# Two last units turned on TensorE, one product group in another PSUM ring, and a new order table, in an mLSTM and SoLU kernel

## The chip, the cores and the metric

The kernel runs on one core of one Trainium2 chip. The metric is the time of one execution in device microseconds (us), taken as the median of several runs; smaller is better.

## The reference

Two layers follow each other. The first is an mLSTM cell over 4 batches, 8 heads, 768 time steps and a head width of 40; the second is a feed-forward layer on the 3072 resulting rows of 320 numbers.

```python
for t in range(S):                                    # per batch and head
    m_new = np.maximum(f_gate[:, :, t] + m, i_gate[:, :, t])
    f_stab, i_stab = np.exp(f_gate[:, :, t] + m - m_new), np.exp(i_gate[:, :, t] - m_new)
    C = f_stab * C + i_stab * outer(vt, kt)
    n = f_stab * n + i_stab * kt
    y[:, :, t] = sigmoid(o_gate[:, :, t]) * (C @ qt) / np.maximum(np.abs(n @ qt), 1.0)
x = y.transpose(0, 2, 1, 3).reshape(B * S, H * D)     # 3072 x 320
h = x @ w_in                                          # 320 -> 1024
solu = h * softmax(h)
ln = (solu - mean(solu)) / np.sqrt(var(solu) + 1e-6) * g_ln
out = ln @ w_out                                      # 1024 -> 320
```

## The kernel before

**Units.** The 768 steps are cut into 6 chunks of 128. A unit is one chunk of one batch, with all 8 heads: 24 units, ordered by chunk and inside a chunk by batch. So unit u needs the state that unit u - 4 left. Inside a chunk the recurrence is written as attention: scores of the chunk's own keys, a decay matrix, and a term from the state.

**One unit, step by step, with the names used below.** TensorE multiplies keys and queries (line 1280, tile `sy`, called e). VectorE multiplies the scores by the decay matrix `d` (line 1293, `p`). TensorE adds the term from the state (line 1320, y.0; VectorE scales it in line 1333) and the products of `p` with the values (line 1347, y.1 and y.2) in one bank. VectorE divides (lines 1363 to 1371, `x`), GpSimd multiplies by the output gate (line 1383), ScalarE takes a row sum of magnitudes (1392), VectorE a scale (1398, 1399), and ScalarE and GpSimd split the row into two fp16 halves `xq` (1453 to 1467). A DMA transpose turns `xq` to `xT` (line 1481). TensorE forms h in `ph` (lines 1497 and 1511, called ph.0 to ph.3). VectorE takes the maximum (1527, `nm`; 1534, `nh`), ScalarE the exponentials (1541), VectorE the product (1559), and ScalarE and VectorE write the centred result as a high and a low fp16 half, `us` (1595 and 1602). `us` is turned into `big`: in units 0 to 22 by one DMA transpose (line 1611), in unit 23 alone by TensorE, 8 transposes for each half (line 1476) into a bank of the ring `sy`, which VectorE (high half, 1626) and ScalarE (low half, 1624) copy to `big`. TensorE multiplies by the output weights: 24 matmuls of 320 columns (line 1664, so.0 to so.3, six each) into the bank `so_`. ScalarE scales the result (line 1680, `ot`) and a DMA stores it (1685).

**PSUM.** The ring `sy` has three banks, in which e, y and the turned halves take turns by a place number; `ph` has two buffers of two banks; `so_` has one bank, which the state updates (line 1416) and the output products share. A group of output products can start only when ScalarE has taken the one before out of that bank.

**The weights.** In the first 75 us the float64 words of both weight matrices are decoded on ScalarE and VectorE (lines 792 to 827), scaled by a bound found through a TensorE transpose (lines 893 and 1031; VectorE's part of the second begins in line 1026, `wmx`), and split into a high and a low fp16 part (lines 935 to 945, 1060 and 1070, `wol`).

**The order.** Every step is a numbered operation of a `Plan`. The table `ORDER` gives the sequence in which all operations are issued, so it fixes the order on each engine and on SP, which issues all DMAs. A pair `(a, b)` interleaves the matmuls of two TensorE operations, and a triple `(a, -1, n)` puts n idle matmuls ahead of a. An engine runs its own operations strictly in that sequence and waits, with all that stands behind, until the inputs of the next one are there. State and value products of the first 6 units that are not in a pair also get an idle matmul beside each step (line 1705).

Of the kernel before, what the change touches and what calls it, by code (L numbers as in the profile page):

```python
# [39 lines left out]
def gdv(P):  # L40
# [433 lines left out]
def mlstm_moe_kernel(ctx: ExitStack, tc: tile.TileContext, tok, qkT, og, fi0, fg, ig, w_in, w_out, gln, out):  # L474
    nc = tc.nc
    units = unit_order()
    NU = len(units)
# [8 lines left out]
    P = Plan()  # L486
# [630 lines left out]
    def unit(u):  # L1117
# [17 lines left out]
        def bank(name, at, ring="sy"):  # L1135
            k = (ring, (name, u))
            P.place[k] = u + at
            return k
# [439 lines left out]
        def uTv(P, a):  # L1578
            return P[uT].bitcast(F16)[:, 0 : 2 * DFF].rearrange("p (a k l) -> p a k l", a=2, l=L)[:, a]


        last = u == NU - 1
        mu = ("mu", u)
        op(
            DVE,
# [173 lines left out]
```

## Time and profile before

| what | us |
|---|---|
| median of 3 runs | 292.49 |
| the three runs | 290.56, 292.49, 297.13 |
| the profiled execution | 291.3 |
| its span | 289.6 |
| TensorE (PE) busy | 275.9 (95%) |
| VectorE (DVE) busy | 231.4 (80%) |
| ScalarE (ACT) busy | 218.3 (75%) |
| GpSimd (POOL) busy | 165.4 (57%) |

The span runs from the first to the last instruction of the profiled execution; its time is 1.7 us longer. PE is TensorE's matmuls, PEld its weight loads, SP the engine that issues the DMAs. A matmul's end is modelled, so TensorE counts as busy through gaps shorter than its pipeline. A time that names a moment is counted from the start of the span.

### The profile page before, as it was taken

Reading aid. Unit: us, or ns where it says so; the run is one execution under the profiler, and the core shown is the slowest. Engines: PE = TensorE matmul, PEld = TensorE weight load, DVE = VectorE, ACT = ScalarE, POOL = GpSimd, SP = SyncE. Lnnn points to the kernel's source line nnn. Section 1 sums busy time; section 2 is a strip of 40 time slices with the busy share of each in tenths; the row PEclk is TensorE's granted clock in tenths of the full one; section 3 lists DMA queues with packets and bytes.
Section 4 is the critical chain, followed back from the end, with each engine's and each line's share of the span. In section 5 each row is a group of like instructions: output and inputs, shape, how many; then the busy total and the mean of one; then the engine's idle time right before and its main releaser. Section 6 shows DMA issues by size and latency. Waiting matters only on the chain.

```text
span 289.6 us, 6648 instructions
## 1 busy us (share of the span) xinstructions
PE 275.9 (95%) x2299; PEld 214.1 (74%) x2299; DVE 231.4 (80%) x611; ACT 218.3 (75%) x472; POOL 165.4 (57%) x275
## 2 busy tenths in 40 slices
PE   6999798998999999999999999999999999989884
PEld 6977787776868878767778777887887767755563
DVE  1999997999988799968789769988897996749720
ACT  2489968989399987799576749997988559466632
POOL 5005879856377388876754476489277326643050
PEclk9999999999999999999999999999999999999999
DMA  7999968587999999699999999969958996496531
GB/s 192 326 336 370 273 169 235 192 244 167 265 221 198 278 261 263 143 239 182 279 252 240 200 288 206 208 161 240 262 177 189 194 231 123 100 155 131 118 79 45
DMA packets 87521, 61.02 MB, mean 211 GB/s; under 512 B 70096, under 2 KB 77392, under 8 KB 87488
## 3 DMA queue, kind: packets, MB, share of 16 engines
q1 hardware_dynamic: 87488, 60.61, 86.3%
q8 instruction: 18, 0.29, 0.4%
q14 instruction: 15, 0.12, 0.1%
HBM read 39.16 MB, written 4.26 MB: 150 GB/s over the span
## 4 chain that ended last, share of the span: by engine, by line
PE 65%; DVE 15%; issue 8%; POOL 4%; ACT 4%; DMA 4%; ACTq 0%; POOLq 0%; DVEq 0%
PE ph L1511 20%; PE sy L1347 6%; PE sy L1280 6%; PE sy L1320 4%; DVE p L1293 3%; DMA big<-us 2%; PE ph L1497 2%; ACT d L1211 2%; DMA xT<-xq 1%; DVE wol L1070 1%; DVE wg L816 1%; DVE wg L827 1%; PE so__4047 L1664 1%; PE so__4086 L1664 1%; PE so__3556 L1664 1%
## 5 line engine op out<-in xcount | busy, mean ns | idle before, releaser
L1664 PEld LDWEIGHTS <-big 128*128 128x128 f16 x576 | 63.2, 116 | 20.5 <-issue 2.4
L1347 PEld LDWEIGHTS sy<-tk,p 128*128 128x128 f32 x384 | 58.0, 193 | 8.9 <-DVE p L1293 2.1
L1511 PE MATMUL ph<-wih,xT 128*128 128x512 f16 x192 | 60.3, 380 | 0.0
L1347 PE MATMUL sy<-tk,p 128*128 128x41 f32 x384 | 57.2, 242 | 2.7 <-DVE p L1293 1.7
L1211 ACT ACTIVATE d<-gb,bG 128x128 f32<-128x128 f32 x160 | 50.0, 391 | 2.4 <-POOL kt L1262 2.4
L1511 PEld LDWEIGHTS <-xT 128*128 128x128 f16 x336 | 36.9, 114 | 18.8 <-issue 2.8
L1511 PE MATMUL ph<-wil,xT 128*128 128x512 f16 x144 | 48.5, 380 | 0.0
L1460 POOL TENSOR_TENSOR xs<-x,xr 128x320 f32<-128x320 f32 x24 | 18.4, 768 | 32.0 <-DVE xr L1399 22.0
L1383 POOL TENSOR_TENSOR x<-x,sg 128x320 f32<-128x320 f32 x24 | 21.7, 905 | 25.8 <-DVE x L1371 15.4
L1541 ACT ACTIVATE e<-ph,nh,hs 128x1024 f32<-128x1024 f32 x24 | 28.7, 1198 | 8.4 <-DVE nh L1534 8.3
L1559 DVE SCALAR_TENSOR_TENSOR e<-ph,s,e 128x1024 f32<-128x1024 f32 x24 | 30.7, 1281 | 4.8 <-ACT e L1541 4.3
L1527 DVE TENSOR_REDUCE nm<-ph 128x1 f32<-128x1024 f32 x24 | 29.2, 1216 | 4.6 <-PE ph L1511 4.6
L1293 DVE TENSOR_TENSOR p<-sy,d 128x512 f32<-128x512 f32 x48 | 32.1, 683 | 0.8 <-POOL d L1233 0.3
L1602 DVE SCALAR_TENSOR_TENSOR us<-e,mu,us 128x1024 f16<-128x1024 f32 x24 | 31.7, 1320 | 0.3 <-ACT us L1595 0.3
L1320 PEld LDWEIGHTS sy<-C,qk 128*128 128x128 f32 x160 | 28.0, 190 | 4.8 <-issue 1.3
L1595 ACT ACTIVATE us<-e,mu 128x1024 f16<-128x1024 f32 x24 | 27.4, 1142 | 2.8 <-DVE mu L1587 2.8
L1320 PE MATMUL sy<-C,qk 128*128 128x82 f32 x160 | 27.6, 260 | 0.7 <-DVE x L1371 0.7
L1569 ACT ACTIVATE sq<-e,a 128x1024 bf16<-128x1024 f32 x24 | 27.4, 1141 | 0.0
L1280 PE MATMUL sy<-qk 64*128 64x128 f32 x384 | 27.3, 281 | 0.0
L1467 POOL TENSOR_TENSOR xq<-xs,xq 128x256 f16<-128x256 f32 (+1 forms) x48 | 25.6, 554 | 2.3 <-ACT xq L1453 1.6
L1280 PEld LDWEIGHTS sy<-qk 64*128 64x128 f32 x384 | 23.8, 187 | 3.3 <-issue 1.7
L1196 POOL TENSOR_SCALAR_AFFINE_SELECT gb<-gb 128x1024 f32<-128x1024 f32 x20 | 22.7, 1133 | 3.3 <-DMA gb<-gd 3.2
(268 smaller groups left out, 614.5 us busy)
## 6 DMA issues: line engine op xcount, KB each, us to landing
gb<-gd SPq DMA_DIRECT2D x20, 512.0 KB, 4.7
qk<-in_qkT_dram SPq DMA_DIRECT2D x21, 448.0 KB, 5.4
tk<-in_tok_dram SPq DMA_DIRECT2D x24, 324.0 KB, 3.8
sg<-in_og_dram SPq DMA_DIRECT2D x12, 320.0 KB, 7.2
out_dram<-ot SPq DMA_DIRECT2D x24, 160.0 KB, 3.6
big<-in_w_in_dram SPq DMA_DIRECT2D x5, 512.0 KB, 7.1
big<-in_w_out_dram SPq DMA_DIRECT2D x4, 640.0 KB, 4.8
qk<-in_qkT_dram SPq DMA_DIRECT2D x3, 512.0 KB, 6.8
```

Of the source, the lines that this page charges most:

```text
L1211: nc.scalar.activation(out=P[d_t][:, j, n, :], in_=P[gb][:, h, :], func=AF.Exp, bias=P[BG][:, 0, c - 1, b * H + h : b * H + h + 1],)
L1280: nc.tensor.matmul(P[ps[j]][:, n * L : (n + 1) * L], lhsT=P[qk][r, 1, n, :], rhs=P[qk][r, 0, n, :], start=True, stop=True,)
L1293: lambda P, j=j: V.tensor_tensor(out=P[p_t][:, j], in0=P[ps[j]].rearrange("p (n l) -> p n l", l=L), in1=P[d_t][:, j], op=ALU.mult,),
L1320: nc.tensor.matmul(P[yk][:, n * 2 * E1 : (n + 1) * 2 * E1], lhsT=P[qk][:, 0, n, :], rhs=P[old][:, n, :], start=first_of_bank(), stop=False ...
L1347: nc.tensor.matmul(yv(P)[:, h, :], lhsT=P[p_t][:, j, n, :], rhs=v1(P)[:, h, :], start=first_of_bank(), stop=True, skip_group_check=True,)
L1511: nc.tensor.matmul(P[ph][:, j * 512 : (j + 1) * 512], lhsT=P[xT][:, a, :], rhs=P[w][:, k, j * 512 : (j + 1) * 512], start=False, stop=n == 6,)
L1527: lambda P: V.tensor_reduce(out=P[nm], in_=P[ph], axis=AX.X, op=ALU.max, negate=True),
L1541: lambda P: nc.scalar.activation(out=P[e], in_=P[ph], func=AF.Exp, bias=P[nh], scale=P[hs], accum_out=P[z]),
L1559: lambda P: V.scalar_tensor_tensor(out=P[e], in0=P[ph], scalar=P[s2], in1=P[e], op0=ALU.mult, op1=ALU.mult, accum_out=P[a]),
L1569: lambda P: nc.scalar.activation(out=P[sq], in_=P[e], func=AF.Square, bias=P[a], scale=-float(DFF), accum_out=P[su]),
L1602: lambda P: V.scalar_tensor_tensor(out=P[us][:, 1], in0=P[e], scalar=P[mu], in1=P[us][:, 0], op0=ALU.add, op1=ALU.subtract),
L1664: nc.tensor.matmul(P[po][:, 0:DM], lhsT=uTv(P, a)[:, k, :], rhs=P[w][:, k, :], start=n == 0, stop=n == 23)
```

## The change

Units 22 and 23 are both turned by TensorE; before, unit 22 was turned by a DMA. Unit 23's output products go to a bank of the ring `sy`, so they no longer wait for unit 22's to leave the bank `so_`. The place numbers of the turned halves are moved so that they fall in sequence. `ORDER` is another list throughout; its first rows stand here for the whole.

```diff
 ORDER = [
-    202, 34, 250, 5, 3, 0, 18, 297, 17, 19, 40, 46, 2, 31, 132, 155, 52, 1, 4, 136, 35, 7, 58, 8, 6, 11, 20, 41, 9,
+    3, 34, 297, 155, 5, 32, 17, 250, 18, 0, 40, 6, 1, 46, 31, 132, 19, 52, 4, 58, 35, 7, 8, 36, 20, 41, 37, 11, 9, 21,
...
-        last = u == NU - 1
+        last = u >= NU - 2
...
-                up = bank(f"t{a_}", 0.4 + 0.1 * a_)
+                up = bank(f"t{a_}", NU - 1 - u + 0.4 + 0.1 * a_ + (0.2 if u == NU - 1 else 0.0))
...
-        po, ot = (("so_", u), ("ot", u))
-        P.place[po] = u + 4.5
+        ot = ("ot", u)
+        po = bank("po", 0.9) if u == NU - 1 else ("so_", u)
+        if u < NU - 1:
+            P.place[po] = u + 4.5
...
+                name="so_",
```

On TensorE the sequence from unit 7 to unit 21 stays nearly the same. At the end it was: products of unit 20, of unit 21, high half of unit 23 turned, products of unit 22, low half of unit 23 turned, products of unit 23. Now it is: products of unit 20, both halves of unit 22 turned, products of unit 21, both halves of unit 23 turned, and then the products of units 22 and 23 six by six among each other (22, 23, 22, 23, 23, 22, 22, 23). The four quarters of unit 19's products, which stood between the four parts of unit 23's h, now stand ahead of them.

VectorE at the very start of the program, where `gb` holds the gates of the first chunk (loaded by a DMA) and `ident` is made by GpSimd. Before:

```order
L563 SCALAR_TENSOR_TENSOR gb<-gb 128x128
L577 TENSOR_TENSOR gb<-gb 128x127
L548 TENSOR_REDUCE dl<-ident 128x8
L555 TENSOR_REDUCE ra<-ident 128x1
L555 TENSOR_REDUCE rb<-ident 128x1
L601 TENSOR_TENSOR gb<-gb 128x128
```

VectorE at the same place now:

```order
L548 TENSOR_REDUCE dl<-ident 128x8
L555 TENSOR_REDUCE ra<-ident 128x1
L555 TENSOR_REDUCE rb<-ident 128x1
L563 SCALAR_TENSOR_TENSOR gb<-gb 128x128
L577 TENSOR_TENSOR gb<-gb 128x127
L800 TENSOR_SCALAR e<-wt 128x512
```

The three sums over `ident` moved ahead of the scan of the gates.

VectorE around the bound of the output weights (`wmx`), where `wg` is the last part of those weights to be decoded and `C` the state. Before:

```order
L827 SCALAR_TENSOR_TENSOR wg<-big,wg 128x640
L1398 TENSOR_SCALAR xm<-xm 128x1
L1399 RECIPROCAL xr<-xm 128x1
L1405 TENSOR_SCALAR hs<-xm,iwi 128x1
L1445 COPY C_72<-so__549 40x4x41
L1026 TENSOR_REDUCE wmx<-wm 128x1
```

VectorE at the same place now:

```order
L827 SCALAR_TENSOR_TENSOR wg<-big,wg 128x640
L1445 COPY C_483<-so__474 40x4x41 x2
L1363 TENSOR_SCALAR rd<-sy 128x8
L1364 TENSOR_TENSOR rd<-sy,rd 128x8
L1365 RECIPROCAL rd<-rd 128x8
L1398 TENSOR_SCALAR xm<-xm 128x1
L1399 RECIPROCAL xr<-xm 128x1
L1371 TENSOR_TENSOR x<-sy,rd 128x320
L1293 TENSOR_TENSOR p<-sy,d 128x512 x2
L1445 COPY C_82<-so__547 40x4x41
L1026 TENSOR_REDUCE wmx<-wm 128x1
```

The decoding of the last part moved ahead of unit 2's division, of unit 3's two score products and of the states of units 1 and 2.

ScalarE at the end of the program, where `ot` with a number is the scaled output of units 20 to 23 in turn. Before:

```order
L1680 ACTIVATE ot<-so__3934,so 128x320
L1569 ACTIVATE sq,su<-e,a 128x1024
L1595 ACTIVATE us<-e,mu 128x1024
L1569 ACTIVATE sq,su<-e,a 128x1024
L1680 ACTIVATE ot<-so__3983,so 128x320
L1680 ACTIVATE ot<-so__4047,so 128x320
L1624 COPY big<-sy 128x1024
L1680 ACTIVATE ot<-so__4086,so 128x320
```

ScalarE at the same place now:

```order
L1569 ACTIVATE sq,su<-e,a 128x1024 x2
L1541 ACTIVATE e,z<-ph,nh,hs 128x1024
L1683 ACTIVATE ot<-so__3930,so 128x320
L1595 ACTIVATE us<-e,mu 128x1024
L1683 ACTIVATE ot<-so__3995,so 128x320
L1624 COPY big<-sy 128x1024
L1569 ACTIVATE sq,su<-e,a 128x1024
L1624 COPY big<-sy 128x1024
L1683 ACTIVATE ot<-so__4064,so 128x320
L1683 ACTIVATE ot<-sy,so 128x320
```

A second copy of a turned half stands behind unit 21's output, and the squares of units 21 and 22 moved ahead of unit 23's exponentials.

## Rows read from the trace of the kernel before

**Rows 1.** Busy time by stretch: us, PE, PEld, DVE, ACT, POOL, granted clock, DMA, GB/s.

```profile
30.00:73.00 43.00, 38.39 (x364) 31.55 (x363) 39.75 (x106) 37.09 (x88) 32.86 (x42) 1.00 0.78 210
73.00:254.00 181.00, 180.52 (x1504) 139.76 (x1503) 151.37 (x414) 142.70 (x314) 113.67 (x191) 1.00 0.96 216
254.00:273.00 19.00, 18.19 (x115) 10.72 (x114) 13.12 (x36) 12.06 (x20) 6.19 (x12) 1.00 0.62 131
273.00:286.50 13.50, 11.17 (x88) 7.87 (x87) 4.03 (x9) 6.14 (x10) 4.14 (x8) 1.00 0.32 77
```

**Rows 2.** Waits of PE from 24 to 73: who waited for whom, total, times, longest.

```profile
PE sy L1347 <- DVE p L1293: 1.7, 2, 1.3
PE ph L1031 <- DVE wmx L1028: 1.1, 1, 1.1
PE sy L1320 <- DVE x L1371: 0.7, 1, 0.7
PE sy L1347 <- DVE sy L1333: 0.7, 2, 0.4
```

**Rows 3.** Waits of PE from 254 to the end.

```profile
PE so__4047 L1664 <- DMA big<-us: 1.0, 1, 1.0
PE so__3983 L1664 <- ACT ot L1680: 0.8, 1, 0.8
PE ph L1497 <- DMA xT<-xq: 0.8, 1, 0.8
PE so__4086 L1664 <- ACT ot L1680: 0.2, 1, 0.2
```

**Rows 4.** Timeline, DVE at the start: start, us, engine, line, operation, [idle before <- releaser].

```profile
6.03 0.42 DVE L563 TENSOR_TENSOR_SCAN gb<-gb 128x128 f32<-128x128 f32 x1 [6.03 <-DMA gb<-in_fi_dram]
...
6.70 0.26 DVE L548 TENSOR_REDUCE dl<-ident 128x8 f32<-128x64 f32 x1
...
7.06 0.28 DVE L601 TENSOR_TENSOR gb<-gb 128x128 f32<-128x128 f32 x1
...
24.15 0.69 DVE L1293 TENSOR_TENSOR p<-sy,d 128x512 f32<-128x512 f32 x1 [0.33 <-POOL d L1233]
```

**Rows 5.** Timeline, DVE from 42 to 68.

```profile
42.16 1.47 DVE L827 SCALAR_TENSOR_TENSOR wg<-big,wg 128x640 int32<-128x640 int32 x1
...
44.58 0.16 DVE L1026 TENSOR_REDUCE wmx<-wm 128x1 f32<-128x4 f32 x1 [0.36 <-ACT wj L1008]
...
47.85 0.51 DVE L1333 TENSOR_TENSOR sy<-sy,bG 128x328 f32<-128x328 f32 x1 [1.20 <-PE sy L1705]
...
67.34 1.38 DVE L1070 SCALAR_TENSOR_TENSOR wol<-wg,gs,woh 128x320 f16<-128x320 f32 x1
```

**Rows 6.** The chain that ended last, its end: start, us, what.

```profile
272.45 6.06 DMA big<-us
278.56 3.45 PE so__4047 L1664 x24
282.08 0.54 ACT ot L1680
282.66 3.43 PE so__4086 L1664 x24
286.25 0.53 ACT ot L1680
```

**Rows 7.** Timeline, all engines, from 269 to 283.

```profile
269.52 0.30 PE L1664 MATMUL so__3934<-woh,big 128*128 128x320 f16 x1
...
271.11 1.28 DVE L1602 SCALAR_TENSOR_TENSOR us<-e,mu,us 128x1024 f16<-128x1024 f32 x1
...
276.95 0.61 PE L1476 MATMUL sy<-ident,us 128*128 128x128 f16 x8
...
277.60 0.69 DVE L1626 COPY big<-sy 128x1024 f16<-128x1024 f16 x1 [0.23 <-PE sy L1476]
...
282.50 1.00 ACT L1624 COPY big<-sy 128x1024 f16<-128x1024 f16 x1
```

126 rows, old and new, of the table ORDER are left out of this document.

## The prediction

> **What bounds the kernel now.** I read the busy time by stretch first [rows 1]. From 73 to 254 TensorE is busy for 180.52 of 181.0 us: there is nothing to take in this stretch but TensorE's own work, and the change leaves that work alone. Only three stretches have room. From 30 to 73 TensorE is idle for 43.00 - 38.39 = 4.6 us while VectorE is busy for 39.75, so VectorE limits the start. From 254 to 273 TensorE is idle for 0.8 us, and from 273 to 286.5 for 13.50 - 11.17 = 2.3 us, of which some 0.3 lie behind its last matmul. The views of waits name the causes. At the start TensorE waits for VectorE's score products (1.7 us in two waits, one of 1.3), for the bound of the output weights (1.1), for unit 6's division (0.7, `x`) and for the scaling of the state term (0.7) [rows 2]. At the end it waits for the DMA that turns unit 22 (1.0), for ScalarE to empty the one bank of output products (0.8 and 0.2) and for one `xT` (0.8) [rows 3]. So if every wait after 30 us went, and 1.2 us of new work (below) came in, the gain would be 4.6 + 0.5 + 0.8 + 2.0 - 1.2 = 6.7 us. With 0.5 us by which the first score product can start earlier, that is the floor: 291.3 - 7.2 = 284.1 us. The reader should keep this small number in mind: a new order for 1340 operations cannot give more than this.
>
> The sums are made against the profiled execution's 291.3 us. It lies 1.2 us below the median of the three runs, 292.49, and 0.7 above the lowest.
>
> **The start of the program.** VectorE waited 6.03 us for the gates' DMA, and then did three sums over `ident` between the scan of the gates and its next step: they begin at 6.70 and the next step begins at 7.06 [rows 4]. Now they stand ahead of the scan and fall into the wait, since `ident` is long made. That takes 7.06 - 6.70 = 0.36 us out of the path to the first score product, which at 24.15 also waited 0.33 us for GpSimd [rows 4]. The set of VectorE operations ahead of that product is the same in both orders, and the last decoding step that ScalarE must see before it makes the first decay matrix stands earlier in VectorE's row. I take 0.5 us; the bounds are 0 (ScalarE or the loads are late instead) and 0.36 + 0.33 = 0.7.
>
> **The bound of the output weights.** Before, the last decoding step ran from 42.16 for 1.47 us, ScalarE had to sum its result, and VectorE waited 0.36 us for that sum at 44.58 [rows 5]. TensorE stood still for 1.1 us because its next operation needs this bound [rows 2], and as its row is strict, unit 4's state term came late and VectorE then waited 1.20 us for it at 47.85 [rows 5]. Now two score products (0.69 us each [rows 4]), a division and copies of two states stand between the decoding step and the bound, where four short steps stood, so VectorE comes to the bound at least 1.4 us later after the decoding and ScalarE's sum is ready. The bound itself has four steps fewer ahead of it and one more. What hides ScalarE's sum is this VectorE work; if ScalarE slipped by over 1 us, the 0.36 us would come back. I take the whole 1.1 us of TensorE's wait, bounds 0 and 1.1 + 0.4.
>
> **From 45 to 73.** VectorE has one `wol` step fewer ahead of unit 6's division, a step that took 1.38 us at that place [rows 5], and one row scale fewer; so the wait of 0.7 us for that division [rows 2] should go. The step comes back right behind, ahead of unit 7's products, but there TensorE has output products to do. The two waits of 0.7 us for the scaling, and what is left of the 1.7 us for score products, I leave standing: VectorE is still the limit there. Unit 4's state update is now interleaved with a part of h, which saves four idle matmuls; TensorE waits in this stretch anyway, so I count nothing. Sum of the start: 0.5 + 1.1 + 0.7 = 2.3 us, bounds 0 and 4.6 + 0.7 = 5.3.
>
> **The stretch from 73 to 254.** TensorE's row is nearly the same, and so are the distances in it between a unit's last value product, its h and its output products. VectorE, ScalarE, GpSimd and SP are reordered throughout. Here I count 0, with bounds of -0.5 (both of its small waits go) and +4 (the rival below). At 256 TensorE waited 0.8 us for unit 22's `xT` [rows 3]. Two quarters of unit 17's output products (12 matmuls, 1.6 us) moved behind the first part of that h, so TensorE asks for this `xT` 1.6 us sooner; against that the output of unit 16, which ScalarE must finish ahead of unit 22's `xq`, can start sooner too, since its last products moved ahead of two parts of unit 21's h. I take no change, with 0.8 us either way.
>
> **The end.** The work that TensorE does ahead of unit 20's output products is the same set in both orders, so I start at 269.52 [rows 7]. One matmul of the products comes every (3.45 - 0.30) / 23 = 0.137 us [rows 6, 7]. Before: 96 of them are 13.15 us, two turned halves of 0.61 each [rows 7] are 1.2; 269.52 + 14.4 = 283.9, but the last group ended at 282.66 + 3.43 = 286.1 [rows 6]: 2.2 us of waits, of which rows 3 name 1.0 + 0.8 + 0.2. Now: 13.15 plus four halves, 2.4, give 285.1, if nothing waits. Each group after unit 20's has 1.2 us of transposes ahead of it, which cover ScalarE's 0.54 us for emptying the bank [rows 6]; the DMA of 6.06 us [rows 6] is gone from this path, and with it one transpose from SP's row, in which four stores stood behind it. Unit 23's products have a bank of their own.
>
> What may be late instead: unit 22's low half, which VectorE began at 271.11 and finished 1.28 us later [rows 7], is asked for at about 269.5 + 3.3 + 0.6 = 273.4; in the new row the short steps for unit 23 come first, and about 0.5 us of margin is left. Unit 23's group waits for a bank of the ring that ScalarE frees with its 1.00 us copy [rows 7], behind unit 21's output; that copy ends within some 0.2 us of the time at which the bank is asked for, and behind the waiting matmuls stands all the rest of unit 22. I allow 0.1 us for both: a gain of 286.1 - 285.1 - 0.1 = 0.9 us, bounds -1.0 (a slip of one ScalarE operation on each group) and 1.0. The last output (0.53 us) and its store follow as before.
>
> **Sum.** 291.3 - 2.3 - 0.9 = 288.1 us for an execution like the profiled one, 289.3 on the scale of the median. I forecast 288.6, between the two.
>
> **A rule that speaks against the turn on TensorE.** The rows show that 8 transposes took 0.61 us and that TensorE's granted clock was 1.00, the upper level of 2.4 GHz, through the whole stretch from 273 to 286.5, although TensorE both waited and turned two halves there [rows 1, 7]. The Trainium skill ("TensorE: Matmul & The Clock Gate", Part 4: PE-mode transpose) says that transposes do not count as activity for the clock in the same way as matmuls, and that one of 128x128 took 275 to 390 ns where it was measured. By its 275 ns the four halves would cost an estimated 8.8 us; by the row they cost 2.4, and this trace does not agree with the page's duration. What it says of the clock is a rival below, since the change doubles the transposes.
>
> **Rivals.**
> - *The start does not move (0.20).* VectorE is 92% busy from 30 to 73 [rows 1]: the waits could only change their names, with the bound's 1.1 us turning up as waits for score products. Against it: the bound's wait is one of order, not of work. Then only the end's gain is left: 290.4 us, 291.6 on the median's scale.
> - *Nearly all waits go (0.17).* For it: they are waits of order, each named in rows 2 and 3. Against it: VectorE's share. 285.0 us, 6.3 below the profiled execution.
> - *A new wait in the full stretch (0.08).* From 73 to 254 TensorE has no slack, so a wait that the new rows of SP or ScalarE put ahead of every unit's `xT` or decay matrix adds up over some 17 units. SP issues strictly in sequence, and several `xT` now stand behind a store or a load of other units. For it: the one late `xT` cost 0.8 us [rows 3]. Against it: TensorE's own distances are kept. From 3.2 / 17 = 0.19 us a unit the whole gain is lost; at 0.5 us a unit the time is 288.1 + 8.5 = 296.6, slower than before.
> - *The clock falls at the end (0.04).* If the two batches of 16 transposes let TensorE's clock drop to its lower level of 1.2 GHz, the last 48 products would take 48 x 0.137 = 6.6 us more, an estimate: 294.7 us, slower than before. Against it: the granted clock stayed at 1.00 through waits and transposes [rows 1]. The page of the Trainium skill named above is what speaks for it.
>
> **How the numbers follow.** The forecast has 0.51, and its own range is 286.5 to 291.0. A measurement of this kernel can tell about 2% from no change: 286.6 and 298.3 on the median of 292.49. Faster by over 2% takes nearly all waits (0.17) and a little of the forecast's lower edge, and some of the former miss it: 0.17. Slower by over 2% needs a new wait of over 0.6 us a unit, or a fallen clock on top of a start that got slower: 0.04. Within 2%: 0.79. The range leaves out the tails of both: 285.0 to 293.0.
>
> **What would show it.** Right: VectorE's first sums ahead of 6.03; no wait of TensorE for the bound near 45; unit 20's products beginning 2 to 2.5 us earlier than 269.5; from there to the last output 0.9 us less; no `big` transpose of unit 22 and no wait for `ot` between groups. Wrong: a TensorE busy time from 73 to 254 that falls below its share now, a granted clock under 1.00 in the last 15 us, or a wait of TensorE for ScalarE's copy in line 1624.

## The result and the profile after

The changed kernel takes 288.13 us in the median of five runs (287.49 to 289.02), the kernel before 292.49. The ratio is 0.990, with a 95% interval of 0.986 to 0.994. The ratio leaves the slowest executions of the kernel before (295 us and more) out, which is why it lies nearer to 1 than the 0.985 of the two medians. So the gain is 1%, clear of none by its interval, and within the 2% either way to which the prediction gave 0.79. The forecast was 288.6. The profiled execution took 288.02 us, against 291.3, and its span fell from 289.6 to 286.3.

Busy time by stretch after the change, which answers to [rows 1] (us, PE, PEld, DVE, ACT, POOL, granted clock, DMA, GB/s):

```profile
30.00:73.00 43.00, 40.10 (x377) 33.10 (x378) 38.27 (x108) 38.52 (x91) 32.99 (x42) 1.00 0.83 224
73.00:254.00 181.00, 179.94 (x1498) 139.08 (x1496) 150.39 (x415) 143.21 (x316) 119.02 (x194) 1.00 0.95 216
254.00:273.00 19.00, 19.00 (x136) 12.19 (x134) 15.11 (x37) 12.02 (x21) 5.41 (x11) 1.00 0.47 106
273.00:286.50 13.50, 9.73 (x82) 7.04 (x79) 2.88 (x5) 5.56 (x8) 4.23 (x8) 0.99 0.11 39
```

TensorE is idle for 2.9 us from 30 to 73, where it was 4.6. From 254 to 273 nothing is left of 0.8. From 73 to 254 its idle time rose from 0.5 to 1.06 us. VectorE is busy for 1.5 us less from 30 to 73, though it does nearly the same set of steps there (108 instructions, before 106); the sixth experiment shows where most of that comes from.

The waits of PE from 24 to 73 us, which answer to [rows 2]:

```profile
PE so__405 L1416 <- DVE bG L728: 1.0, 1, 1.0
PE sy L1320 <- DVE x L1371: 0.8, 1, 0.8
PE so__474 L1416 <- DVE C L1445: 0.4, 1, 0.4
PE sy L1347 <- DVE sy L1333: 0.3, 1, 0.3
...
PE sy L1347 <- DVE p L1293: 0.2, 1, 0.2
```

The wait for the bound (`wmx`) is gone and so is most of that for the score products. Two new ones stand in their place, for `bG` (1.0) and for a state copy (0.4), and the wait for unit 6's division (`x`) is still there. Two more are new in the stretch from 73 to 254:

```profile
PE ph L1497 <- DMA xT<-xq: 0.6, 1, 0.6
PE so__1210 L1666 <- DVE C L1443: 0.5, 1, 0.5
```

From 254 us to the end the view of waits names none; [rows 3] had 2.8 us there. The end of the chain that ended last, which answers to [rows 6] (start, us, what):

```profile
267.79 3.26 PE so__3930 L1666 x24
271.05 1.01 PE sy L1476 x16
272.05 3.26 PE so__3995 L1666 x24
275.31 0.89 PE sy L1476 x16
276.21 0.81 PE so__4064 L1666 x6
277.02 0.81 PE sy L1666 x6
...
281.91 0.83 PE sy L1666 x6
```

It is TensorE alone: unit 20's products, unit 22's two halves turned in 1.01 us, unit 21's products, unit 23's halves in 0.89 us, and the products of units 22 and 23 by turns. Unit 20's first product starts at 267.62:

```profile
267.62 0.30 PE L1666 MATMUL so__3930<-woh,big 128*128 128x320 f16 x1
```

VectorE at the start, which answers to [rows 4]:

```profile
2.94 0.26 DVE L548 TENSOR_REDUCE dl<-ident 128x8 f32<-128x64 f32 x1 [2.94 <-POOL ident masks.py:199]
...
5.39 0.42 DVE L563 TENSOR_TENSOR_SCAN gb<-gb 128x128 f32<-128x128 f32 x1 [2.01 <-DMA gb<-in_fi_dram]
...
24.20 0.69 DVE L1293 TENSOR_TENSOR p<-sy,d 128x512 f32<-128x512 f32 x1 [0.53 <-PE sy L1280]
```

The three sums do stand ahead of the scan, but the first score product starts at 24.20, where it was 24.15. It now waits for TensorE's scores and no longer for GpSimd. The gates' load landed 0.64 us sooner in this execution (the scan begins at 5.39 instead of 6.03); in the other profiles with the new start the scan begins at 5.88 to 6.56, so it is this execution and not the change.

With these rows the 3.35 us between the two traces can be laid out. I take moments at which both kernels begin the same piece of work. The first score product is at +0.05. Unit 4's scores begin at 43.98 instead of 45.31, so that -1.38 comes between these two (VectorE's row does not hold quite the same steps between them: 45 instructions instead of 50). Unit 8's scores stand at -1.35, units 20 to 22 at -0.98, so that 0.37 is lost in the full stretch. Unit 20's first output product is at -1.90 (267.62 against 269.52): 0.92 more, where the wait for unit 22's `xT` was. From there to the end of the last output product it takes 15.12 us instead of 16.57, another -1.45.

### The profile page after: what moved, and what is told of

Same layout as the page of the kernel before. It is cut to its first block, busy times and chain, and to the rows that moved or that the text cites. A ratio compares the mean times of both kernels' runs of the same rounds, so it can differ in the third digit from the quotient of the medians.

```text
span 286.3 us, 6662 instructions
## 1 busy us (share of the span) xinstructions
PE 275.6 (96%) x2309; PEld 214.7 (75%) x2309; DVE 230.0 (80%) x612; ACT 219.4 (77%) x473; POOL 171.9 (60%) x275
## 4 chain that ended last, share of the span: by engine, by line
PE 76%; DVE 16%; DMA 2%; issue 2%; POOL 2%; ACT 1%; DVEq 0%; ACTq 0%; POOLq 0%
PE ph L1511 20%; PE sy L1347 7%; PE sy L1280 6%; PE ph L1704 5%; PE sy L1320 4%; DVE p L1293 2%; DMA xT<-xq 2%; DVE wol L1070 2%; PE ph L1497 2%; DVE nm L1527 2%; DVE us L1602 1%; PE so__1210 L1666 1%; PE so__2043 L1666 1%; PE so__3567 L1666 1%; PE so__3306 L1666 1%
## 5 line engine op out<-in xcount | busy, mean ns | idle before, releaser
L1511 PE MATMUL ph<-wih,xT 128*128 128x512 f16 x192 | 61.0, 380 | 0.0
L1541 ACT ACTIVATE e<-ph,nh,hs 128x1024 f32<-128x1024 f32 x24 | 28.7, 1194 | 10.3 <-DVE nh L1534 10.3
L1602 DVE SCALAR_TENSOR_TENSOR us<-e,mu,us 128x1024 f16<-128x1024 f32 x24 | 32.9, 1370 | 2.2 <-ACT us L1595 2.1
L1460 POOL TENSOR_TENSOR xs<-x,xr 128x320 f32<-128x320 f32 x24 | 21.4, 892 | 20.4 <-DVE xr L1399 15.9
L1467 POOL TENSOR_TENSOR xq<-xs,xq 128x256 f16<-128x256 f32 (+1 forms) x48 | 26.7, 577 | 6.5 <-issue 3.5
L1196 POOL TENSOR_SCALAR_AFFINE_SELECT gb<-gb 128x1024 f32<-128x1024 f32 x20 | 21.9, 1097 | 3.0 <-DMA gb<-gd 2.9
```

Of the source, the lines that this page charges most:

```text
L1511: nc.tensor.matmul(P[ph][:, j * 512 : (j + 1) * 512], lhsT=P[xT][:, a, :], rhs=P[w][:, k, j * 512 : (j + 1) * 512], start=False, stop=n == 6,)
L1541: lambda P: nc.scalar.activation(out=P[e], in_=P[ph], func=AF.Exp, bias=P[nh], scale=P[hs], accum_out=P[z]),
L1602: lambda P: V.scalar_tensor_tensor(out=P[us][:, 1], in0=P[e], scalar=P[mu], in1=P[us][:, 0], op0=ALU.add, op1=ALU.subtract),
```

## The experiments

In the tables of the order an edit stands here as rows of the engine whose order it changes. In the profiles of the first four kernels the line numbers lie one to four lower than in the changed kernel.

**1. The end alone, and all but the end.**

```diff
 ORDER = [
-    (new order up to unit 20's so.0)
+    (old order up to unit 20's so.0)
     (new order from there)
```

> The changed code, with the order of the kernel before up to unit 20's first output product and the new order behind it. Theory: the four stretches are separate, so this keeps the old start, the old wait for unit 22's xT and unit 20's products at about 269.5 us, and takes only the end's 1.5 us: 289.8 us for an execution like the profiled 291.3, a ratio of 0.995, and 15.1 us from unit 20's first product to the last output product. Rival: the end is only short because the units 21 to 23 came early in the new order, so that here TensorE waits for unit 22's halves or for the copies of the bank: under 0.5 us gained, ratio 0.998 to 1.003, 16 us or more from unit 20's products to the end.

Measured: 290.17 us, ratio 0.995 (0.992 to 0.998). From unit 20's first product (270.74) to the end of the last one (285.88) it takes 15.14 us, the changed kernel's 15.12. Unit 20's products began later than expected, for in this execution the scores of unit 0 waited for their load:

```profile
PE sy L1279 <- DMA qk<-in_qkT_dram: 1.4, 1, 1.4
```

The rival falls: the end's gain needs nothing of the new order ahead of it.

The counterpart is the code of the kernel before with the two parts the other way round.

> The code of the kernel before (unit 22 turned by the DMA, unit 23's products in the shared bank), with the new order up to unit 20's first output product and the old one behind it. Theory: the start's 1.2 us and the 0.9 us of the wait for unit 22's xT come, less 0.2 lost between: unit 20's products begin at 267.7, the end takes 16.6 us as before, 289.4 us for an execution like the profiled 291.3, ratio 0.993. Rival: the DMA that turns unit 22 and ScalarE's row hold the old end where it was, so that an earlier start turns into a longer wait for that DMA: the end takes 17.5 us or more, and the ratio is 0.998 or more.

Measured: 290.0 us, ratio 0.991 (0.987 to 0.995); unit 20's products at 267.36, and 16.56 us from there to the end. The waits of PE after 254 us are those of [rows 3], without the one for `xT` (the third, of 0.2 us, is there too):

```profile
PE so__4042 L1663 <- DMA big<-us: 1.0, 1, 1.0
PE so__3978 L1663 <- ACT ot L1679: 0.8, 1, 0.8
```

So the new order and the new end are two separate gains that add up.

**2. The two parts of the end.** First the turn without the bank, then the bank without the turn:

```diff
-        po = bank("po", 0.9) if u == NU - 1 else ("so_", u)
-        if u < NU - 1:
-            P.place[po] = u + 4.5
+        po = ("so_", u)
+        P.place[po] = u + 4.5
```

> The changed kernel, but unit 23's products go to the shared bank, all 24 behind all 24 of unit 22, as one group waits for ScalarE to empty the bank: the turn by TensorE alone. Theory: one emptying of the bank (0.54 us) and its two handshakes stand between unit 22's last product and unit 23's first: 0.8 us more than the changed kernel, 288.9 us, and one wait of TensorE for ot of 0.8. Rival: the bank is worth nothing, since the six-by-six sequence only spreads the same work: within 0.2 us of the changed kernel.

Measured: 289.03 us, ratio 0.988 (0.980 to 0.996); the end takes 16.03 us, 0.91 more than in the changed kernel. The one wait of PE after 254 us is the expected one:

```profile
PE so__4100 L1664 <- ACT ot L1681: 0.8, 1, 0.8
```

```diff
-        last = u >= NU - 2
+        last = u == NU - 1
```

> The changed kernel, but unit 22 is turned by the DMA as before; unit 23's products keep their bank and the six-by-six sequence: the bank alone. Theory: unit 22's low half is ready at about 270.5 us, SP's row and the transfer take 6 us, so big lands at 276.5 to 277; without the 1.0 us of unit 22's transposes TensorE is through unit 21's products at about 274.4 and unit 23's halves at 275.3 to 277.0; it waits 0.5 to 2 us for big, less the 1.0 saved: 287.7 to 289 us, a loss of at most 1 us against the changed kernel. Rival: the DMA turn is hidden by the reordered products and TensorE saves its 1.0 us: 287.0 us or less.

Measured: 289.23 us, ratio 0.989 (0.982 to 0.996); the end takes 15.79 us, 0.67 more than in the changed kernel. In the chain that ended last the transfer stands where the turn was:

```profile
271.87 5.22 DMA big<-us
```

It lands at 277.09. Against the old end (16.57) the turn alone is worth 0.54 us, the bank alone 0.78, both 1.45. Neither is worth nothing, and each takes a wait out that the other leaves: in the bank alone TensorE still waits 0.8 us for ScalarE ahead of unit 21's products and 0.6 us for this transfer, in the turn alone 0.8 us ahead of unit 23's. The 289.23 us lies just above the 287.7 to 289 that were expected.

**3. Four repairs of single waits.** If each wait of TensorE at the start is a matter of order, removing one should pay. First, fewer idle matmuls ahead of the transpose that takes the bound of the input weights:

```diff
-    (65, -1, 8)
+    (65, -1, 1)
```

> The changed kernel with one idle f32 matmul instead of eight ahead of the transpose that takes the bound of the input weights (line 893), near 21 us; nothing else. Theory: VectorE came to the first score product about 0.5 us early, and TensorE's 16 idle matmuls (20.95 to 22.90 us) held back the bound and the scores; with 7 of them fewer (0.12 us each) unit 0's scores begin at 22.1 and the first score product at 23.4 instead of 24.2 us, of which 0.3 to 0.8 us reach unit 20's products. Rival: the queries and keys, or GpSimd's decay matrix, come no sooner, or VectorE limits what follows: the first score product within 0.2 us, or the gain is gone by unit 4's scores.

Measured: 294.51 us (292.93 and 296.10), ratio 1.011 (0.987 to 1.035). ScalarE and GpSimd were late in this execution (GpSimd's first decay matrix began at 22.59, not 21.81), so the moments cannot be compared directly; counted from that decay matrix, the first score product came after 1.78 us instead of 2.39. The theory was right there. But the granted clock fell. Busy time of this kernel from 32 to 34 us (the granted clock is the third number from the end):

```profile
32.00:34.00 2.00, 2.00 (x14) 2.00 (x14) 1.62 (x4) 1.97 (x3) 1.71 (x1) 0.50 1.00 264
```

Its timeline shows what TensorE did before that:

```profile
31.48 0.38 PE L1416 MATMUL so__398<-tk,kt 128*104 128x82 f32 x2 [1.63 <-DVE bG L728]
```

TensorE stood still for 1.63 us, waiting for `bG`, and from 32 us on its granted clock was 0.50, the lower level of 1.2 GHz, until about 42. In the changed kernel the same wait is 1.0 us and the clock stays at 1.00. Between unit 1's and unit 3's scores 4.5 us were lost. Both executions of this kernel had a mean granted clock of 0.982 or less; the other kernels with the new start had 0.997 or more. So the idle matmuls that cost 0.6 us of the start also stand for more than that.

Second, VectorE's step on `bG` at its old place:

```diff
 L1293 TENSOR_TENSOR p<-sy,d 128x512
+L728 TENSOR_TENSOR bG<-bG,so__209 128x160 x2
 L800 TENSOR_SCALAR wg<-wt 128x640 x2
...
-L728 TENSOR_TENSOR bG<-bG,so__209 128x160 x2
 L1371 TENSOR_TENSOR x<-sy,rd 128x320
```

> The changed kernel with VectorE's second step on the gates' tile bG (line 728, 0.63 us) right behind unit 0's second score product, where it stood in the kernel before, instead of behind unit 0's division. Theory: the new wait of 1.0 us of TensorE at 30.8 us (unit 0's state update for bG) goes, and measured from the first score product units 2 to 4 begin 0.5 to 1.0 us sooner. Rival: VectorE limits this stretch, so the wait only turns into one for unit 1's score products: under 0.2 us.

Measured: 288.56 us, ratio 0.981 (0.968 to 0.993). The wait for `bG` is gone from the view of waits, and these two grew, from 0.4 and from 0.2:

```profile
PE so__474 L1416 <- DVE C L1445: 1.1, 1, 1.1
...
PE sy L1347 <- DVE p L1293: 0.6, 1, 0.6
```

Unit 4's scores follow the first score product by 20.05 us, against 19.78 in the changed kernel. The rival holds: nothing is gained.

Third, unit 6's division ahead of the state copy and the mean:

```diff
+L1363 TENSOR_SCALAR rd<-sy 128x8
...
+L1371 TENSOR_TENSOR x<-sy,rd 128x320
 L1443 TENSOR_TENSOR C_797<-C_797,so__867 40x4x41
 L1587 TENSOR_SCALAR mu<-a 128x1
-L1363 TENSOR_SCALAR rd<-sy 128x8
```

> The changed kernel with unit 6's division (lines 1363 to 1371) ahead of unit 4's second state copy and unit 1's mean (C, mu) in VectorE's row near 67 us. Theory: it was these two and not the step of the low output weights that kept the division late; the wait of TensorE for x near 70.6 (0.8 us) falls to 0.3 or less, and from unit 7's scores on the kernel is 0.3 to 0.6 us earlier. Rival: the division waits for TensorE's own products of unit 6, so the wait stays at 0.6 or more.

Measured: 288.56 us, ratio 0.986 (0.976 to 0.996). The wait for `x` is gone, but unit 8's scores begin 55.59 us behind the first score product, in the changed kernel 55.61: a wait of 0.4 us for line 1333 that was not there has come ahead of them, and nothing is gained. Unit 16's `xT`, which came 0.6 us late in the changed kernel, came 1.4 us late here and not at all in two other profiles with the changed kernel's order up to there (the order alone and the bank alone).

Fourth, the two new waits of the full stretch:

```diff
 L1443 TENSOR_TENSOR C_754<-C_754,so__1109 40x4x41
+L1443 TENSOR_TENSOR C_754<-C_754,so__1109 40x4x41
...
-L1443 TENSOR_TENSOR C_754<-C_754,so__1109 40x4x41
```

and on TensorE unit 16's first part of h behind unit 19's scores.

> The changed kernel with unit 5's second state copy right behind the first in VectorE's row (near 83 us) and with unit 16's first part of h behind, not ahead of, unit 19's scores in TensorE's row (near 196 us). Theory: the two new waits of the full stretch (0.5 us for C at 83.4, 0.6 us for unit 16's xT at 196.3) go, and nothing takes their place: unit 20's products 0.9 to 1.1 us earlier against the first score product. Rival: the first only moves on to unit 2's exponentials and the second to unit 19's scores: under 0.3 us.

Measured: 288.81 us, ratio 0.983 (0.977 to 0.990). Both waits are gone. Unit 9's scores gain 0.45 us and unit 10's lose 0.8, in a wait that was not there before:

```profile
PE so__1402 L1666 <- DVE C L1443: 0.7, 1, 0.7
```

Unit 6's state copy stood in VectorE's row behind unit 3's sum `ab`, which waits 1.1 us for GpSimd. Unit 20's products follow the first score product by 243.33 us, against 243.42. So here too a repaired wait of TensorE came back under another name.

**4. The load of the first keys.**

```diff
 L994 DMA big<-in_w_out_dram 128x2x640
+L1145 DMA qk<-in_qkT_dram 128x1024
 L1141 DMA tk<-in_tok_dram 128x648
 L994 DMA big<-in_w_out_dram 128x2x640
-L1145 DMA qk<-in_qkT_dram 128x1024
```

> The kernel before with one transfer moved in SP's row: the load of unit 0's queries and keys (line 1145) stands ahead of the load of unit 1's tokens and of the second part of the output weights, as in the new order, so that SP issues it at about 12.7 us instead of 16.5. Nothing else. Theory: in executions of the kernel before in which this load lands late (1.4 us of TensorE waiting at 24 us in one profile, none in the other), TensorE stands still, and sometimes its granted clock falls as in the run with fewer idle matmuls; with the earlier load the median falls from 292.5 to about 291.3 us, the span of times from 290.8 - 295.7 to within 2.5 us, and no execution has a mean granted clock under 0.99. Rival: the spread comes from the loads of the weights, which gate ScalarE: times and clocks spread as before, median 292 or more.

Measured: 292.2 us (289.29 to 297.29, 12 runs), ratio 0.996 (0.992 to 1.001); three of the 12 executions had a mean granted clock of 0.977 to 0.988. The theory falls: the spread of the old order does not come from this load. What it comes from is open, since none of the executions of the old start that were profiled had a low clock. In 51 executions with the new order of the start (all kernels here but those with the old start and the one with fewer idle matmuls) the mean granted clock was 0.997 or more; in the 10 of the end alone, which has the old start, it was 0.994 or more. Of 56 executions of the kernel before that were timed beside the experiments, 13 had a mean of 0.977 to 0.983 and took 294.4 us or more; one fall as long as that of the third experiment gives such a mean (0.982 in its profile), so a fall of that kind is likely, but where it stands in the program is not shown.

**5. VectorE's own waits.** Four of its steps were moved into waits of VectorE, not of TensorE:

```diff
+L1398 TENSOR_SCALAR xm<-xm 128x1
+L1399 RECIPROCAL xr<-xm 128x1
 L1363 TENSOR_SCALAR rd<-sy 128x8
...
+L1445 COPY C_82<-so__547 40x4x41
+L1398 TENSOR_SCALAR xm<-xm 128x1
+L1399 RECIPROCAL xr<-xm 128x1
 L1363 TENSOR_SCALAR rd<-sy 128x8
...
+L1070 SCALAR_TENSOR_TENSOR wol<-wg,gs,woh 128x320
 L1398 TENSOR_SCALAR xm<-xm 128x1
```

> The changed kernel with four of VectorE's steps moved into waits of its own between 39 and 51 us: unit 0's and unit 1's row scales ahead of the divisions of units 2 and 3, a copy of unit 2's state ahead of the latter too, and one step of the low output weights ahead of unit 2's row scale, which waits for ScalarE. No TensorE wait is touched. Theory: from 45 to 90 us VectorE is the limit, so work put into its own waits is gained: 0.25 + 0.6 + 0.7 = 1.5 us of its waits go, and measured from the first score product unit 8's scores and unit 20's products come 0.8 to 1.5 us earlier; median 287.0 us. Rival: TensorE's row limits, as its waits were only shuffled: under 0.3 us.

Measured: 288.12 us, ratio 0.985 (0.978 to 0.992). VectorE's waits in the changed kernel, from 39 to 52 us, and in this one (timeline rows, the wait in brackets):

```profile
39.61 0.17 DVE L1363 TENSOR_SCALAR rd<-sy 128x8 f32<-128x8 f32 x1 [0.58 <-PE sy L1708]
43.97 0.17 DVE L1363 TENSOR_SCALAR rd<-sy 128x8 f32<-128x8 f32 x1 [1.05 <-PE sy L1708]
47.05 0.16 DVE L1049 COPY iw<-ph 128x1 f32<-128x1 f32 x1 [0.25 <-PE ph L1042]
50.68 0.15 DVE L1398 TENSOR_SCALAR xm<-xm 128x1 f32<-128x1 f32 x1 [1.15 <-ACT xs L1392]
```

```profile
40.03 0.17 DVE L1363 TENSOR_SCALAR rd<-sy 128x8 f32<-128x8 f32 x1 [0.20 <-PE sy L1708]
44.40 0.17 DVE L1363 TENSOR_SCALAR rd<-sy 128x8 f32<-128x8 f32 x1 [0.44 <-PE sy L1708]
47.47 0.16 DVE L1049 COPY iw<-ph 128x1 f32<-128x1 f32 x1 [0.73 <-PE ph L1042]
50.71 0.15 DVE L1398 TENSOR_SCALAR xm<-xm 128x1 f32<-128x1 f32 x1 [0.18 <-ACT xs L1392]
51.86 0.17 DVE L1363 TENSOR_SCALAR rd<-sy 128x8 f32<-128x8 f32 x1 [0.35 <-PE sy L1347]
```

Four waits of 3.0 us became five of 1.9. Unit 8's scores follow the first score product by 55.54 us; in the changed kernel by 55.61, and in the turn alone, which has the changed kernel's row of VectorE but the same wait of 1.3 us for `bG` as this one, by 55.90. The gain is 0.1 to 0.4 us, under what the theory said and close to the rival. At unit 20's products, the theory's second mark, nothing of it is left against the changed kernel (243.46 us behind the first score product, 243.42 there; 243.89 in the turn alone). VectorE and TensorE wait for each other by turns here; neither alone is the limit.

Then all the moves together, and unit 3's `ab` behind unit 6's second state copy, so that this copy is not stuck:

```diff
-L1643 TENSOR_SCALAR ab<-ab,su 128x1
 L1398 TENSOR_SCALAR xm<-xm 128x1
 L1399 RECIPROCAL xr<-xm 128x1
 L1443 TENSOR_TENSOR C_1291<-C_1291,so__1334 40x4x41
+L1643 TENSOR_SCALAR ab<-ab,su 128x1
```

> The changed kernel with the four moves into VectorE's waits, unit 5's second state copy right behind the first, unit 3's sum ab (which waited 1.1 us for GpSimd at 94.9) behind unit 6's second state copy, and unit 16's first part of h behind unit 19's scores. Theory: 0.8 to 1.5 us from VectorE's waits, 0.4 from the wait for C at 83 us, which now finds no copy that is stuck behind ab, and 0.4 to 0.6 from unit 16's xT: 285.8 to 286.5 us, against 288.1 of the changed kernel. Rival: a wait removed in the full stretch comes back one unit later, as with unit 5's copy alone: 287 us or more.

Measured: 287.99 us (287.51 to 288.22), ratio 0.984 (0.978 to 0.990). Its median is the lowest of all, but 0.14 us under the changed kernel's is not told apart from none. In the trace unit 20's products follow the first score product by 242.32 us instead of 243.42, so 1.1 us was gained. But 0.47 of that came by unit 4's scores (19.30 against 19.77), and hardly by the moves, with which alone it was 20.11: GpSimd waited 1.02 us for a load of tokens at 35 us in this execution, and the VectorE step beside it took 0.82 us instead of 1.36, for which the sixth experiment has the reason. The first score product was 0.96 us later in this execution (25.16); over the profiles with this start it lies anywhere from 24.06 to 25.50. Unit 10 gained 1.4 us, and 0.7 was lost again right behind it:

```profile
PE so__1480 L1416 <- ACT ot L1683: 0.6, 1, 0.6
```

There ScalarE does the sigmoid of eight units' gates (line 1249) ahead of unit 2's output, so that TensorE now runs into ScalarE's row.

**6. The idle matmuls moved into a wait.**

```diff
-    (65, -1, 8)
+    (65, -1, 4)
...
-    (154, -1, 1)
+    (154, -1, 5)
```

> The kernel called combined with TensorE's idle matmuls shared out otherwise: 4 instead of 8 ahead of the transpose for the bound of the input weights (near 22 us), and 5 instead of 1 ahead of unit 0's state update (near 31 us), where TensorE waits for VectorE's step on bG; nothing else. Theory: the first score product follows GpSimd's first decay matrix 0.8 us sooner (1.6 us behind its start instead of 2.4), the wait for bG is filled, so the granted clock stays at 1.00 where it fell to 0.50 with fewer idle matmuls; unit 20's products come 0.3 to 0.8 us sooner, counted from the start of GpSimd's first decay matrix, and the median is 287.2 to 287.7 us. Rival A: ScalarE's sigmoid ahead of unit 2's output (a wait of 0.6 us at 101 us) takes what the start gives: within 0.2 us of combined, 287.9. Rival B: the clock falls in some executions all the same: 291 us or more in these.

Measured: 288.73 us, ratio 0.988 (0.985 to 0.991). The six executions took 287.91, 287.93, 288.13, 289.33, 289.33 and 289.37 us, and the profile is of the last. The first score product follows the start of GpSimd's decay matrix by 1.78 us, not 2.42, and the granted clock stays at 1.00 in the profiled execution. Yet unit 20's products come 1.14 us later, counted from the same point (245.88 against 244.74). Neither rival had this; the first three times are those of combined (rival A), the other three are not, and none of the first three was profiled. VectorE's row is that of the kernel called combined, step for step, but its steps take longer. The steps that decode the output weights (`wg`), from 19 to 45 us, in the kernel before, the changed kernel and this one (busy us, mean ns | idle before):

```profile
L827 DVE SCALAR_TENSOR_TENSOR wg<-big,wg 128x640 int32<-128x640 int32 x4 | 4.6, 1159 | 0.0
L816 DVE SCALAR_TENSOR_TENSOR wg<-big,wg 128x640 int32<-128x640 int32 x4 | 4.6, 1149 | 0.0
L800 DVE TENSOR_SCALAR wg<-wt 128x640 int32<-128x640 int32 x4 | 2.3, 582 | 0.0
```

```profile
L827 DVE SCALAR_TENSOR_TENSOR wg<-big,wg 128x640 int32<-128x640 int32 x4 | 3.8, 950 | 0.0
L816 DVE SCALAR_TENSOR_TENSOR wg<-big,wg 128x640 int32<-128x640 int32 x4 | 3.2, 818 | 0.0
L800 DVE TENSOR_SCALAR wg<-wt 128x640 int32<-128x640 int32 x4 | 2.8, 728 | 0.0
```

```profile
L827 DVE SCALAR_TENSOR_TENSOR wg<-big,wg 128x640 int32<-128x640 int32 x4 | 4.8, 1189 | 0.0
L800 DVE TENSOR_SCALAR wg<-wt 128x640 int32<-128x640 int32 x4 | 3.4, 862 | 0.0
L816 DVE SCALAR_TENSOR_TENSOR wg<-big,wg 128x640 int32<-128x640 int32 x4 | 3.2, 816 | 0.0
```

Four times the three means, the same twelve steps take 11.6, 10.0 and 11.5 us, and 9.5 in the kernel called combined. The timeline says when a step is long. In combined and in this kernel, VectorE's step of line 827 and the GpSimd step near it:

```profile
32.51 0.81 DVE L827 SCALAR_TENSOR_TENSOR wg<-big,wg 128x640 int32<-128x640 int32 x1
...
32.84 1.49 POOL L942 TENSOR_TENSOR wil<-e,wih 128x512 f16<-128x512 f32 x1 [1.36 <-ACT wih L945]
```

```profile
32.79 1.63 DVE L827 SCALAR_TENSOR_TENSOR wg<-big,wg 128x640 int32<-128x640 int32 x1
...
32.58 1.16 POOL L942 TENSOR_TENSOR wil<-e,wih 128x512 f16<-128x512 f32 x1 [0.81 <-ACT wih L945]
```

Where VectorE begins first, its step takes 0.81 us and GpSimd's 1.49. Where GpSimd begins first, by 0.2 us, it takes 1.16 and VectorE's 1.63. The one that comes second waits for the other. VectorE's step that came second ended 0.68 us behind GpSimd's, not much less than the 0.81 that it takes by itself. Over the profiles such a step grows with what is left of GpSimd's step when it begins, less about 0.1 us: 0.95 us left made it 0.82 longer, 0.69 made 0.55, 0.22 made 0.10 (the latter two in the kernel before, at 32.57 and 34.31). And TensorE, which had waited 0.2 us for the score product behind this step in combined, waited here:

```profile
PE sy L1347 <- DVE p L1293: 1.0, 1, 1.0
```

The Trainium skill ("Trainium Architecture — The Big Picture", "What this means for kernel authors") says that on the engines' side of SBUF only the pair of ports shared by VectorE and GpSimd contends, and that it is an exclusive lock and not a split of the bandwidth. On the lock the rows of line 827 and line 942 agree (1.63 us against 0.81 for the second); that nothing else contends no run here shows. Across the profiles (the names are those of the experiments; "bG early" is the second repair, "division first" the third, "mid waits" the fourth):

| kernel | the twelve steps, us | first score product to unit 4's scores, us |
|---|---|---|
| before | 11.6 | 21.16 |
| keys early (old order) | 11.5 | 21.05 |
| idle matmuls moved | 11.5 | 20.92 |
| end alone (old order) | 11.2 | 20.82 |
| order alone, turn alone, VectorE filled | 10.3 | 20.11, 20.06, 20.11 |
| bG early | 10.1 | 20.05 |
| changed kernel, bank alone, division first, mid waits | 10.0 | 19.78, 19.77, 19.76, 19.77 |
| combined | 9.5 | 19.30 |

Only the kernel whose clock fell is left out. Over the table one microsecond of these steps is 0.8 to 0.9 us of this stretch. Three of the kernels have one and the same row of VectorE there, and differ all the same: combined, VectorE filled and idle matmuls moved, with 9.5, 10.3 and 11.5 us of steps and 19.30, 20.11 and 20.92 us for the stretch. From the kernel before to the changed one the steps fell by 1.6 us and the stretch by 1.38.

## Why the prediction was right, and where it was not

The time was right (288.1 us for an execution like the profiled one, measured 288.02) because misjudged terms cancelled, and that is luck: the start gave 1.35 us instead of 2.3, the full stretch took 0.37 back, and the end with unit 22's `xT` gave 2.37 instead of 0.9. The first score product alone begins anywhere from 24.06 to 25.50 us in the profiles with the new start, so that two single executions agree to 0.1 us with the sum is luck as well.

- **Start of the program, -0.5: wrong, 0.** The sums did move into the wait, and GpSimd's first decay matrix began 1.07 us sooner (21.81 against 22.88). Of that, 0.64 us is the gates' load that landed sooner in this execution; from the scan to the decay matrix it takes 16.42 us instead of 16.85, near the 0.36 that I had worked out. The step that failed is that the product waits only for VectorE and GpSimd: 16 idle f32 matmuls of TensorE, 1.95 us, stood ahead of the bound and the scores, and the product waited 0.53 us for the scores. The run with fewer of them showed the 0.6 us, and the price.
- **The bound of the output weights, -1.1: right in size, probably wrong in cause.** The wait went, and -1.38 us came by unit 4's scores. I put it down to what stands between the decoding step and the bound. The step that failed is that TensorE's wait, once gone, is time gained. With the same row in VectorE and the same bound, the run with moved idle matmuls is 1.6 us slower over this stretch than combined, because its decoding steps take 2.0 us more; its stretch is only 0.24 us shorter than that of the kernel before (20.92 against 21.16), though the wait for the bound is gone there too, and a wait of 1.0 us for a score product stands in its place. I had read 1.47 us for one of these steps [rows 5] as its duration; the same step took 0.81 us in other places, and the twelve steps fell by 1.6 us in all. So most of the gain goes with these steps. It was not tried to change the meetings of VectorE and GpSimd alone, so that they made the gain is argued and not shown: the table above shows that the two go together in 13 profiles, and the pair of rows shows how a step gets long. Nor was it forecast: which engine begins first was no part of the working.
- **Unit 6's division, -0.7: wrong, 0.** The wait is 0.8 us now. The step that failed is what stands ahead of the division: unit 1's product (1.28 us), a state copy and a mean, not the `wol` step that had gone. VectorE in the changed kernel:

```profile
67.41 1.28 DVE L1559 SCALAR_TENSOR_TENSOR e<-ph,s,e 128x1024 f32<-128x1024 f32 x1
...
68.74 0.33 DVE L1443 TENSOR_TENSOR C<-C,so__867 40x164 f32<-40x164 f32 x1
...
69.28 0.17 DVE L1363 TENSOR_SCALAR rd<-sy 128x8 f32<-128x8 f32 x1
```

- **The stretch from 73 to 254, 0: nearly right, +0.37.** The bounds were -0.5 and +4. The two new waits are single ones (0.5 and 0.6 us), not one per unit as in that rival. TensorE's busy time in this stretch fell from 180.52 to 179.94 us, which the prediction had named as a sign of being wrong; it cost no more than this.
- **Unit 22's `xT`, 0 with 0.8 either way: -0.92, just outside.** The wait went in the changed kernel and in the order alone, and stayed in the end alone (0.8 us); so it was the new order ahead of unit 20's products that made this `xT` early enough.
- **The end, -0.9: right in mechanism, -1.45.** I priced four turned halves at 0.61 us each, from 8 transposes that stood alone. Sixteen in a row took 1.01 and 0.89 us, 0.5 us less in all, and the 0.1 us allowed for waits was not needed.
- **The rivals.** "The start does not move" was half true: it moved by 1.35 us at unit 8's scores, where 2.3 was predicted. "Nearly all waits go" came true at the end alone. The granted clock was 1.00 until the last product, which ended at 282.74; the 0.99 of the last 13.5 us comes from what lies behind it (0.96 from 284.00 to the end):

```profile
282.00:284.00 2.00, 0.73 (x6) 0.29 (x3) 0.00 (x0) 1.06 (x2) 0.00 (x0) 1.00 0.23 81
```

So the 32 transposes did not lower it here, and the rival of the clock did not come true.

## What to carry to other kernels

A wait that has a name is not yet a gain: in a stretch where two engines wait for each other by turns, taking out waits of TensorE (in three experiments here) moved them to a later step, while waits in the tail, where TensorE alone was left, paid and added up. When the same instruction appears with two durations in a timeline, ask which engine began first beside it, before its duration goes into a sum. A kernel whose times fall into two groups, as that of the sixth experiment, is not described by one profile. Idle matmuls have two sides: they hold back what stands behind them, and they may be what keeps the clock up, so that they are better moved into a wait than removed.

## What the runs showed of the hardware

A VectorE step of lines 816 and 827 on 128x640 int32 took 0.80 to 0.83 us alone or when it began before GpSimd's step, and 0.90 to 1.63 us when it began 0.2 us or more behind a GpSimd step that had 0.2 us or more to run. GpSimd's step of line 942 took 1.16 us when it began first, and 1.49 us when it began 0.33 us behind VectorE's. A shift of some tenths of a microsecond decides which engine is first, which makes the start of this kernel sensitive to small changes elsewhere.

TensorE's granted clock fell from 1.00 to 0.50 after a wait of 1.63 us at 30 us, in a start that had also 0.55 us of waiting near 22 us, and was back at 1.00 by 44 us; after waits of 1.0 to 1.3 us at the same place it did not fall in the profiled executions. That one fall cost 4.5 us, more than the change gained between the two profiles (3.35).
